# The last weight set in three transfers instead of one, and fifteen small loads behind it on the same queue

## The chip, the cores and the metric

The kernel runs on one core of a Trainium2 chip. A core has a matrix engine (PE), a vector engine (DVE), an activation engine (ACT), a general engine (POOL) and a sync engine (SP). In this kernel SP computes nothing: it is the queue from which nearly all transfers between memory and the core's buffers are issued, one after the other, and sixteen DMA engines carry them out. The metric is the device time of one execution in microseconds (us), lower is better. Before the change it is 218.73 us, the median of two runs (218.32 and 219.14).

## The reference

Two sequences (B = 2) with one token each go through a gated block. The input row is normalised; one branch is attention over a cached window, the other a gated feed-forward part; the output is the input plus the product of the two.

```python
xn = layernorm(x)                                  # x: 2 x 1 x 512
q = (xn @ wq)                                      # 32 heads of 128
k, v = k_cache[:, :, SK-W:, :], v_cache[:, :, SK-W:, :]   # 8 kv heads, window W = 4096
p = softmax(q k^T * 128**-0.5)                     # 4 query heads share a kv head
s = (p v).reshape(2, 1, 4096) @ wo                 # wo: 4096 x 512
z = gelu(xn @ w_in); z1, z2 = halves(z)
g = silu((z1 * (w_sp * layernorm(z2) + b_sp)) @ w_out)
out = x + s * g                                    # 2 x 1 x 512
```

All of it is in 32-bit floats. What has to be read is far larger than what is computed on it: the window of keys and values alone is 64 MB, wq and wo are 8 MB each.

## The kernel before, in words

**Stages.** The feed-forward branch (`win`, `wout`) and the queries (`wqt`) come first. Then eight units follow, one for each kv head; a unit holds 4 MB of keys (`k`) and 4 MB of values (`v`). DVE turns the keys of a unit in four chunks (`turn`), PE multiplies them with the queries (`scores`), and the softmax (`probabilities`) and the product with the values (`values`) follow one or two units later. The outputs of the units are gathered in three sets (`SETS`, line 332): units 0 to 3, units 4 and 5, and units 6 and 7. Each set ends in a small tile `oT` (`spread`), which is the stationary side of the last product, the one with `wo`.

**The last product.** The rows of `wo` are cut like the sets: 4 MB for the first, 2 MB for the second and 2 MB for the third. Lines 479 to 488 load them into two large buffers as *blocks*: a block is one transfer, with its own completion. Before the change the blocks are two of 2 MB for the first set, one of 2 MB for the second, and four of 1 MB, 512 KB, 256 KB and 256 KB for the third. A block of 2 MB gives eight matrix products, one of 256 KB gives one. The first two sets go through `wo_early` (lines 492 to 500), which sums into the four row groups of `part`, 24 products in all (`EARLY = 24`). ACT copies `part` to `parts`, PE folds its groups into `so` with `rowm`, and the blocks of the third set are added to `so` (lines 520 to 527). Then DVE multiplies `so` by the gate and adds the input (`res`, lines 529 and 530), and SP issues the transfer of the result (line 531).

**What sets the order.** `pe`, `dve`, `act` and `sp` are wrapped in `InOrder`: each engine's instructions stay in the order in which the program writes them. For SP that means that a transfer that must wait holds up every transfer written behind it. A transfer on SP waits for three kinds of things. It waits until its buffer may be overwritten: the large buffers are a ring of four, so a load into one waits for the last reader of what was in it, and a load that overwrites what an earlier load wrote waits until that load has landed. It waits for data that it sends out. And it waits for its completion semaphore: the framework has eight for the transfers of SP and ACT and hands them out in turn, so a transfer that takes a semaphore again waits until the transfer eight places earlier has landed. In the built program of before, the last block of `wo` waits for the values of unit 6 to have landed for this reason, and the result's transfer for those of unit 7.

The packets of everything that SP issues go through one queue to the sixteen DMA engines. `x4` (line 108) is the input, loaded early through ACT, and it is the only other small load of a similar kind beside `xs` and the two scalars of `wb1`.

Of the kernel before, what the change touches and what calls it, by code (L numbers as in the profile page):

```python
# [9 lines left out]
F32 = mybir.dt.float32  # L10
# [4 lines left out]
P = 128  # L15
# [27 lines left out]
def kernel(  # L43
# [14 lines left out]
    pe, dve, act, sp = (InOrder(tc, e) for e in (nc.tensor, nc.vector, nc.scalar, nc.sync))  # L58
# [20 lines left out]
    cst = ctx.enter_context(tc.tile_pool(name="cst", bufs=1))  # L79
# [4 lines left out]
    def slot(name, *shape):  # L84
        return ring.tile([P, *shape], F32, tag="slot", name=name)
# [21 lines left out]
    act.dma_start(wb1[:, 1:2], bass.AP(tensor=b_sp.tensor, offset=b_sp.offset, ap=[[1, 1], [1, 1]]))  # L107
    x4 = cst.tile([P, DC], F32, tag="x4", name="x4")
    nc.gpsimd.memset(x4, 0.0)
    by_group = [[DC, G], [D, B], [1, DC]]  # L110
    act.dma_start(x4[0 : P : P // (G * B), :], bass.AP(tensor=x.tensor, offset=x.offset, ap=by_group))

# [330 lines left out]
    def spread_after(p):  # L443
        if p is not None and p.n in ends:
            spread(ends[p.n])
# [33 lines left out]
    blocks = []  # L479
    for first, of in ((0, (0,)), (1, (1, 2))):  # L480
        t = slot(f"wo{first}", 16, D)
        a = 0
        for i in of:
            nj = SETS[i][2]
            for j, n in (((0, 8), (8, 8)), ((0, 8),), ((0, 4), (4, 2), (6, 1), (7, 1)))[i]:
                sp.dma_start(t[:, a : a + n, :], wo_s[i][:, j : j + n, :])
                blocks.append((t[:, a : a + n, :], sets[f"oT{i}"][1], j))
                a += n
    EARLY = 24
    done = 0  # L490

    def wo_early(n):
        nonlocal done
        t, oT, j = blocks[n]
        for a in range(t.shape[1]):
            g = done % G
            pe.matmul(
                part[32 * g : 32 * g + 32, :], oT[:, j + a, :], t[:, a, :], start=(done < G), stop=(done >= EARLY - G)
            )
            done += 1  # L500
# [9 lines left out]
    wo_early(0)  # L510
    gathered(units[-1])
    spread_after(units[-1])
    wo_early(1)
    wo_early(2)
    parts = sb.tile([P, D], F32, tag="o", name="parts", bufs=1)
    act.activation(parts, part, AF.Copy)
    so = bank("so", DC)
    for g in range(G):
        pe.matmul(so[32 * g : 32 * g + 32, :], rowm, parts[:, g * DC : (g + 1) * DC], start=True, stop=False)
    for n in range(3, len(blocks)):  # L520
        t, oT, j = blocks[n]
        for a in range(t.shape[1]):
            for g in range(G):
                pe.matmul(
                    so[32 * g : 32 * g + 32, :], oT[:, j + a, :], t[:, a, g * DC : (g + 1) * DC],
                    start=False, stop=(j + a == oT.shape[1] - 1),
                )
# [32 lines left out]
```

## Time and profile before

| | |
|---|---|
| median of two runs | 218.73 us (218.32 to 219.14) |
| the profiled execution, its own time | 219.13 us |
| its span, first to last instruction | 217.3 us |
| mean granted TensorE clock | 0.772 |
| PE busy | 144.6 us (67%) |
| DVE busy | 104.3 us (48%) |
| ACT busy | 23.9 us (11%) |
| SP's packets, share of 16 DMA engines | 96.3% |
| read from memory | 89.40 MB, 411 GB/s over the span |

The span runs from the first to the last instruction of the core; the time of the execution is 1.8 us more. A row of the timeline gives the start, the busy time, the engine and what is written from what. A row of the chain of work gives the same for the work that ended last, followed back from the end; "DMA" in it is a stretch in which the next instruction waited for a transfer, counted from the transfer's issue. A row of the waits says which engine waited for which result, how long in total, how often, and the longest one. "SPq" is SP's queue of instructions: its busy time on a transfer is the time to issue it, not the transfer itself.

### The profile page before, as it was taken

The page shows a single profiled execution, that of the slowest core. Times are in us where ns is not written, and L with a number is a line of the kernel's source. Part 1 is how long each engine was busy: PE and PEld are TensorE (multiplying, and loading weights), DVE is VectorE, ACT ScalarE, POOL GpSimd, SP SyncE. Part 2 cuts the span into 40 slices and gives each one's busy share as a digit, 9 for nine tenths or more (in the row PEclk, how much of TensorE's full clock was granted, in tenths as well). Part 3 has the DMA queues.
Part 4 walks back from the last instruction along what each step waited for, and adds up shares of the span by engine and source line. Part 5 has one row for each costly group of instructions (what it writes and reads, how often), then busy time and mean ns, then how long its engine had stood idle before and what let it go on. Part 6 is the DMA issues. An engine that isn't in the chain of part 4 may idle for free.

```text
span 217.3 us, 2319 instructions
## 1 busy us (share of the span) xinstructions
PE 144.6 (67%) x970; PEld 55.6 (26%) x970; DVE 104.3 (48%) x162; ACT 23.9 (11%) x60; POOL 3.2 (1%) x16
## 2 busy tenths in 40 slices
PE   0179694826956956974693197459478669979663
PEld 0128521513112212222231122312121122342213
DVE  2511214359459458638709903980684495221101
ACT  5010203100001101011021002102000012021010
POOL 5000000000000000000000000000000000000000
PEclk9998578785597695595599569857855879988969
DMA  7999999999999999999999999999999999999980
GB/s 254 423 434 464 404 464 401 454 410 440 428 434 431 422 440 416 449 410 446 416 452 410 458 407 446 416 440 425 422 442 416 446 416 452 404 413 431 412 323 2
DMA packets 3929, 89.54 MB, mean 412 GB/s; under 512 B 446, under 2 KB 462, under 8 KB 848
## 3 DMA queue, kind: packets, MB, share of 16 engines
q1 hardware_dynamic: 3900, 89.40, 96.3%
q8 instruction: 7, 0.11, 0.2%
q14 instruction: 2, 0.02, 0.0%
q10 hardware_dynamic: 20, 0.01, 0.0%
HBM read 89.40 MB, written 0.00 MB: 411 GB/s over the span
## 4 chain that ended last, share of the span: by engine, by line
DMA 60%; PE 19%; DVE 17%; SPq 1%; issue 1%; ACT 1%; DVEq 0%; ACTq 0%
DMA v<-in_A_v_cache_dram 29%; DMA k<-in_A_k_cache_dram 20%; DVE kt L37 13%; DMA wo<-in_A_wo_dram 11%; PE acc L37 8%; PE s L37 7%; PE part L37 2%; SPq L37 1%; PE so L37 1%; PE pp L37 1%; DVE sm L37 1%; DVE pT L37 1%; DVE qw L37 1%; ACT p L37 0%; DVE mg L37 0%
## 5 line engine op out<-in xcount | busy, mean ns | idle before, releaser
L37 DVE STREAM_TRANSPOSE kt<-k 128x2048 f32<-128x2048 f32 x32 | 72.7, 2293 | 2.4 <-DMA k<-in_A_k_cache_dram 2.4
L37 PE MATMUL acc<-v,pT 128*32 128x512 f32 x256 | 44.9, 857 | 11.1 <-DMA v<-in_A_v_cache_dram 9.8
L37 PE MATMUL s<-kt,qw 128*32 128x512 f32 x256 | 41.0, 683 | 3.7 <-DVE kt L37 3.1
L37 PE MATMUL pp<-p,swap 128*128 128x512 f32 x16 | 12.8, 898 | 21.0 <-ACT p L37 21.0
L37 DVE CUSTOM_DVE_ANT_1 sm<-s,own 128x512 f32<-128x512 f32 x8 | 5.5, 690 | 36.9 <-PE s L37 36.9
L37 PEld LDWEIGHTS acc<-v,pT 128*32 128x32 f32 x256 | 11.5, 159 | 37.4 <-issue 33.4
L37 PEld LDWEIGHTS s<-kt,qw 128*32 128x32 f32 x256 | 9.4, 122 | 32.8 <-issue 21.7
L37 ACT ACTIVATE o<-acc,wd 128x128 f32<-128x128 f32 x30 | 8.7, 368 | 74.0 <-PE acc L37 67.2
L37 PE MATMUL q_ps<-wq,xnT 128*32 128x512 f32 x64 | 10.2, 767 | 5.3 <-DMA wq<-in_A_wq_dram 5.3
L37 ACT ACTIVATE p<-sm,nb 128x512 f32<-128x512 f32 x8 | 5.8, 723 | 68.1 <-DVE nb L37 68.1
L37 PE MATMUL part<-wo,oT 128*32 128x512 f32 x48 | 7.3, 737 | 2.7 <-DMA wo<-in_A_wo_dram 2.7
L37 PEld LDWEIGHTS pp<-p,swap 128*128 128x128 f32 x16 | 3.0, 234 | 21.8 <-ACT p L37 21.8
L37 DVE STREAM_TRANSPOSE pT<-pp 128x512 f32<-128x512 f32 x8 | 5.7, 706 | 6.0 <-PE pp L37 6.0
L37 PE MATMUL z<-win,xnT 128*32 128x448 f32 x32 | 5.2, 820 | 4.6 <-DMA win<-in_B_w_in_dram 4.6
L37 PE MATMUL mo<-mg,same 128*128 128x16 f32 x16 | 3.2, 273 | 7.7 <-DVE mg L37 7.7
L37 DVE TENSOR_REDUCE both<-col 128x32 f32<-128x128 f32 x3 | 0.9, 292 | 13.3 <-PE col L37 13.3
L37 PE MATMUL zT_ps<-rowm,z 128*128 128x2 f32 x28 | 6.6, 370 | 0.0
L37 PEld LDWEIGHTS zT_ps<-rowm,z 128*128 128x128 f32 x28 | 6.5, 325 | 0.0
L37 PEld LDWEIGHTS mo<-l,same 128*128 128x128 f32 x16 | 4.6, 290 | 6.1 <-issue 6.1
L37 DVE TENSOR_TENSOR res<-so,gate 128x128 f32<-128x128 f32 x1 | 0.3, 292 | 10.7 <-PE so L37 10.7
L37 ACT ACT_TABLE_LOAD x4 | 5.1, 1283 | 2.6 <-POOL place L207 2.6
L37 PEld LDWEIGHTS mo<-mg,same 128*128 128x128 f32 x16 | 2.4, 188 | 11.7 <-DVE mg L37 10.9
(105 smaller groups left out, 71.8 us busy)
## 6 DMA issues: line engine op xcount, KB each, us to landing
k<-in_A_k_cache_dram SPq DMA_DIRECT2D x8, 4096.0 KB, 26.6
v<-in_A_v_cache_dram SPq DMA_DIRECT2D x8, 4096.0 KB, 29.9
wq<-in_A_wq_dram SPq DMA_DIRECT2D x2, 4096.0 KB, 24.5
wo<-in_A_wo_dram SPq DMA_DIRECT2D x3, 2048.0 KB, 19.6
win<-in_B_w_in_dram SPq DMA_DIRECT2D x1, 3584.0 KB, 11.4
wout<-in_B_w_out_dram SPq DMA_DIRECT2D x1, 1792.0 KB, 15.2
wo<-in_A_wo_dram SPq DMA_DIRECT2D x1, 1024.0 KB
wo<-in_A_wo_dram SPq DMA_DIRECT2D x1, 512.0 KB
```

The source lines that it names most:

```text
L37: return self.tc.keep_in_program_order(call(*args, **kwargs))
```

## The change

The transfer of the second set of `wo`, one of 2 MB, becomes three of 1 MB, 512 KB and 512 KB. With it the second set is blocks 2 to 4 in place of block 2, and the third set is blocks 5 to 8. The products stay the same in number, shape and order; `wo_early` runs over blocks 1 to 4 and waits for each of them by itself.

Behind the last block of `wo`, SP issues fifteen loads from the input `x` into the first rows of a new tile `marks`: 15 rows of 64 bytes, then 14 rows, and so on down to one. Nothing reads `marks`. All fifteen write from row 0 of the same tile. The result's transfer (line 531 before) comes behind them on SP.

```diff
+    x_in = x
...
-            for j, n in (((0, 8), (8, 8)), ((0, 8),), ((0, 4), (4, 2), (6, 1), (7, 1)))[i]:
+            for j, n in (((0, 8), (8, 8)), ((0, 4), (4, 2), (6, 2)), ((0, 4), (4, 2), (6, 1), (7, 1)))[i]:
                 sp.dma_start(t[:, a : a + n, :], wo_s[i][:, j : j + n, :])
                 blocks.append((t[:, a : a + n, :], sets[f"oT{i}"][1], j))
                 a += n
+    marks = cst.tile([P, 16], F32, tag="marks", name="marks")
+    for n in range(15, 0, -1):
+        sp.dma_start(marks[:n, :], bass.AP(tensor=x_in.tensor, offset=x_in.offset, ap=[[16, n], [1, 16]]))
...
-    wo_early(1)
-    wo_early(2)
+    for n in range(1, 5):
+        wo_early(n)
...
-    for n in range(3, len(blocks)):
+    for n in range(5, len(blocks)):
```

## The prediction

> **What bounds the kernel now.** I read the page first, for the shares; then the end of the chain of work; then SP's own timeline and waits, because everything that the change adds stands on SP.
>
> From the page:
>
> ```profile
> span 217.3 us, 2319 instructions
> ...
> DMA  7999999999999999999999999999999999999980
> ...
> q1 hardware_dynamic: 3900, 89.40, 96.3%
> ...
> HBM read 89.40 MB, written 0.00 MB: 411 GB/s over the span
> ```
>
> The sixteen DMA engines are full in every slice but the first and the last two, and nearly all of it is SP's queue. So the kernel is as long as its transfers, plus what has to happen after the last of them. A change behind the last transfer is paid in full, unless something else is still running then.
>
> What still runs then is shown by the last eleven pieces of the chain that ended last:
>
> ```profile
> 183.28 24.28 DMA wo<-in_A_wo_dram
> 207.55 0.14 issue
> 207.69 3.52 PE part L37 x16
> 211.21 0.02 issue
> 211.23 0.60 ACT parts L37
> 211.84 0.04 issue
> 211.88 2.22 PE so L37 x72
> 214.10 0.02 issue
> 214.12 0.30 DVE res L37
> 214.43 0.02 issue
> 214.45 0.29 DVE res L37
> ```
>
> The second set of `wo`, issued at 183.28, lands at 207.55. PE's eight products with it take until 211.21, the copy and the third set until 214.10, DVE until 214.74. Then the result can go out.
>
> SP's timeline, and SP's waits from 180 us to the end (who waited for whom, in total, times, longest):
>
> ```profile
> 182.36 3.20 SPq L37 DMA_DIRECT2D wo<-in_A_wo_dram  x7
> 214.77 0.69 SPq L37 DMA_DIRECT2D out_dram<-res  x1
> ```
>
> ```profile
> SPq L37 <- DVE res L37: 22.2, 1, 22.2
> ...
> SPq L37 <- DMA v<-in_A_v_cache_dram: 7.0, 1, 7.0
> SPq L555 <- DMA out_dram<-res: 0.7, 1, 0.7
> ```
>
> All seven transfers of `wo` are issued by 185.56 (182.36 + 3.20). Then SP stands 7.0 us, to about 192.5, until the values of unit 7 have landed, and 22.2 us until `res` is there at 214.77. In those 29 us SP has nothing to do, and this is where the fifteen loads go. Whether they fit there is the question of this case.
>
> When `wo` lands, from the group of its transfers, and how the DMA engines end, from a table of short stretches (the last two columns are the engines' share and GB/s):
>
> ```profile
> L37 SPq DMA_DIRECT2D wo<-in_A_wo_dram x7: 336/426/437, 182.4 to 185.1; - x7
> ...
> DMA to landing us min/median/max: 19.6/27.3/27.5
> ```
>
> ```profile
> 207.50:209.00 1.50, 1.31 (x8) 0.45 (x12) 0.00 (x0) 0.00 (x0) 0.00 (x0) 0.50 0.98 400
> 209.00:210.00 1.00, 1.00 (x8) 0.22 (x4) 0.00 (x0) 0.00 (x0) 0.00 (x0) 0.50 1.00 387
> 210.00:211.00 1.00, 1.00 (x8) 0.00 (x0) 0.00 (x0) 0.00 (x0) 0.00 (x0) 0.56 0.63 240
> 211.00:212.00 1.00, 0.29 (x8) 0.12 (x8) 0.00 (x0) 0.60 (x1) 0.00 (x0) 1.00 0.31 115
> 212.00:213.00 1.00, 1.00 (x41) 1.00 (x41) 0.00 (x0) 0.00 (x0) 0.00 (x0) 1.00 0.01 2
> ```
>
> The last block, only 256 KB, is issued at 185.1 and lands 27.5 us later, at 212.6; the engines are empty at 212. A short transfer takes as long as all that was queued in front of it. That is how a first-come queue looks.
>
> **The change part by part.**
>
> *The waits of the added loads.* In the built program each small load waits for its predecessor to have landed, since both write row 0 of `marks`. The first eight also wait for the transfer eight places earlier, whose semaphore they take: the load of 15 rows for the second block of the first set, that of 14 rows for block 2, and so on to that of 8 rows, for block 8, the last of `wo`. The result's transfer waits for `res` alone, but it stands behind all fifteen on SP. What is queued behind the waiting loads is only that transfer; the end of the kernel waits for it, and nobody else does.
>
> *Blocks 6 to 8 of `wo`.* With two more transfers, three blocks now wait for semaphores: block 6 for the values of unit 6, block 7 for those of unit 7 (192.5), block 8 for the first block of the first set. The second 2 MB block lands at about 202.3 (issued at about 182.7, plus the 19.6), the third at 207.55; so 2 MB take some 5 us, and the first lands at about 197.4. Block 8 is issued then, with 15 us of transfers (197.4 to 212.6) still in the queue. The engines stay full, and this costs nothing; the cover would have to shrink by 15 us before it did.
>
> *The second set in three pieces.* Its last piece lands when the whole did, at 207.55, as the bytes in front are the same. But by then PE has done the first six products instead of none: the 1 MB piece lands some 2.5 us earlier, the next some 1.3 us earlier, and PE is idle there. After 207.55 two products of eight are left, 3.52 × 2/8 = 0.9 us. So `part` ends at about 208.6 instead of 211.21 and `parts` at 209.3. From there the third set binds: its last block lands at 212.6, one product is left of it (2.22 us for 36 products of `so`, so four of them 0.25), and PE ends near 213.0 instead of 214.10. Alone this would be worth about 1.1 us. It is worth nothing if SP isn't free at 213.7.
>
> *The fifteen loads.* The first is issued at 202.3 and queues behind `wo`; by the reading above it lands with the end of `wo`, at 212.6. From there, thirteen loads (14 to 2 rows) follow each other, each issued when the one before has landed. The last, one row, is issued and not waited for; then the result goes out. For the step, from the issue of one to the issue of the next, the trace has no row. The nearest are small transfers on an empty queue. From the first microseconds, and from the closing line of the program (its group on SP; count, then min/median/max ns, first and last start):
>
> ```profile
> 0.74 0.55 ACTq L37 DMA_DIRECT2D xs<-in_A_x_dram  x1
> ...
> 1.32 0.24 ACTq L37 DMA_DIRECT2D wb<-in_B_w_sp_dram  x1
> ...
> 2.16 0.68 DVE L37 BATCH_NORM_STATS2 st<-xs 2x6 f32<-2x512 f32 x1
> ```
>
> ```profile
> L555 SPq DRAIN  x3: 7/7/13, 216.6 to 216.9; - x3
> ```
>
> `xs`, two rows read into the core, is issued at 0.74 and its reader starts at 2.16: 1.42 us. The result, eight rows of 512 bytes written to memory, is issued at 214.77, and SP goes on past its landing at 216.6: 1.83 us. In `xs`, 0.55 is the issue; with the shortest issue of a small load, 0.24, it would be 1.42 − 0.55 + 0.24 = 1.11 us. A step is therefore between 1.11 and 1.83 us by the rows, or longer if there is something in a chain of loads that neither row shows. I take 1.65: the kind of transfer is that of `xs`, but the queue is that of the result, where landing takes longer, and an instruction with a wait stands ahead of each load.
>
> The Trainium skill, "DMA: Bandwidth & Descriptors", section "Anatomy of one DMA — SWDGE (gpsimd) path", gives a fixed cost of about 2.0 us for a transfer on another issue path, most of it the confirmation that the last byte has landed. By that price the sum below would end at 243.4. The trace's own two rows are both shorter.
>
> *The sum.* 212.6 (first load landed) + 13 × 1.65 = 21.45, which is 234.05; + 0.45 for the issue of the last load (the transfers of `wo` take 0.43, the row above) is 234.5, where the result is issued. In the trace it is issued at 214.77 and the span ends at 217.3, 2.53 later; so the new span is 237.0, 19.7 more. The profiled execution takes 219.13, 1.83 over its span, which gives **238.9 us**. That execution is at the upper end of the two runs shown, 0.4 above their median; against the median the forecast would be 238.5, and I keep 238.9.
>
> With the two ends of the step: 1.11 gives 212.6 + 14.4 + 0.24 + 2.53 + 1.83 = 231.6; 1.83 gives 212.6 + 23.8 + 0.69 + 2.53 + 1.83 = 241.5. `res` is ready near 213.7 and waits some 20 us for SP, so the gain of the three pieces is not seen.
>
> **The rivals.**
>
> *The small loads pass the bulk.* If the first of them landed soon after its issue at 202.3, the next six would wait for the blocks one by one (their semaphores), and the load of 8 rows for the last block at 212.6. Then seven steps follow (8 to 2 rows) instead of thirteen: 212.6 + 7 × 1.65 + 0.45 + 2.53 + 1.83 = 229.0. For it: fifteen rows of 64 bytes are few packets. Against it: the 256 KB block that landed with all that stood in front of it, 27.5 us after its issue.
>
> *The step is longer than either row.* Rows of 64 bytes, or the waits for two semaphores ahead of a load, might cost what `xs` and the result don't show. At 2.1 us the time is 244.7, at 2.4 us 248.6. For it: `xs` is issued while SP and ACT have just started, and the result is a single transfer, so neither shows a chain. Against it: both are whole transfers from issue to effect.
>
> *Not slower.* The loads are short and might be hidden: SP is free for 29 us and the result isn't ready before 213.7. The point from which this decides is the first load's landing. If it and the others landed at once and cost their issue alone, eight issues of 0.24 would be left after 212.6, the result would go out at 214.5, and the time would be 218.9, no change. With the chain that the program has, 214.77 − 212.6 = 2.2 us would have to hold thirteen steps, 0.17 us each, a tenth of any row. That the three pieces then gain their 1.1 us, to 218.0, also ends here.
>
> **How the numbers follow.** Chain behind `wo` with a step up to 2.0 us: 0.78. The longer step: 0.13. The small loads pass the bulk: 0.06. Not slower: 0.03. The range goes from 233.5 (a step of 1.25 us, nearer the lower bound than I think likely) to 245.0 (a step of 2.1); it takes in most of the first case and about half of the second. A measurement of this kernel tells some 2%, 4.4 us, from no change; all cases but the last are slower by more than that: slower 0.97, same 0.03 with less than 0.01 for faster.
>
> **What the changed profile would show.** Right: SP's timeline has fifteen issues of `marks`, the first near 202.3, the second near 212.6, the rest at equal distances of 1.4 to 1.9 us; SP waits for `marks` some 15 us in total behind `wo`; the DMA line of the page is empty in its last four slices; PE's last product with `wo` ends near 213.0; the chain that ended last runs over `marks`. Wrong in the first rival's way: several issues of `marks` before 212. Wrong in size: equal distances, but of another length. Wrong altogether: the result issued before 216.

## The result and the profile after

The changed kernel takes 234.58 us (median of two runs, 234.44 and 234.73) beside 218.73 us before: 1.071 times as long, with an interval of 1.064 to 1.078. The forecast was 238.9 us, in a range of 233.5 to 245.0. The direction and the mechanism held, and the result lies in the range, near its lower end; the middle was 4.3 us too long.

The page of the changed kernel, the same lines as quoted of before:

```profile
span 232.7 us, 2342 instructions
...
DMA  7999999999999999999999999999999999992000
...
q1 hardware_dynamic: 4428, 89.41, 90.0%
...
HBM read 89.41 MB, written 0.00 MB: 384 GB/s over the span
```

The bytes are the same but for the 8 KB of the loads, and the DMA engines are as full as before for as long as they have work. The span is 15.4 us longer, and the last three slices, 17 us, are empty: the time has been added *behind* the transfers.

SP's own timeline, from the first transfer of `wo` to the end (start, busy time or, where several are merged, the stretch they cover):

```profile
182.27 15.58 SPq L37 DMA_DIRECT2D wo<-in_A_wo_dram  x9
202.42 27.28 SPq L37 DMA_DIRECT2D marks<-in_A_x_dram  x15
229.75 0.67 SPq L37 DMA_DIRECT2D out_dram<-res  x1
```

The result is issued at 229.75 instead of 214.77. Ahead of it stand the fifteen loads, which take SP from 202.42 to 229.70. What SP does in that time is in its waits (whom it waited for, in total, times, longest), shown first. The timeline in short stretches gives single issues; behind the waits stand those of the loads of 15, 14 and 13 rows and of the last two:

```profile
SPq L37 <- DMA marks<-in_A_x_dram: 20.4, 14, 7.7
...
SPq L37 <- DMA wo<-in_A_wo_dram: 11.2, 3, 4.6
SPq L37 <- DMA v<-in_A_v_cache_dram: 7.2, 1, 7.2
```

```profile
202.42 0.41 SPq L37 DMA_DIRECT2D marks<-in_A_x_dram  x1
212.66 0.32 SPq L37 DMA_DIRECT2D marks<-in_A_x_dram  x1
214.00 0.31 SPq L37 DMA_DIRECT2D marks<-in_A_x_dram  x1
...
228.34 0.23 SPq L37 DMA_DIRECT2D marks<-in_A_x_dram  x1
229.48 0.22 SPq L37 DMA_DIRECT2D marks<-in_A_x_dram  x1
```

SP waits for its own small loads fourteen times. The longest wait, 7.7 us, is the second load's for the first, which queues behind `wo`; the second load is issued at 212.66. Then come thirteen steps in 16.82 us (212.66 to 229.48), 1.29 us each, of which 0.22 to 0.32 is the issue and the rest waiting.

The compute, in the meantime, is done early. The last pieces of the chain that ended last:

```profile
212.52 0.47 PE so L37 x8
212.99 0.02 issue
213.02 0.30 DVE res L37
213.32 0.02 issue
213.34 0.29 DVE res L37
```

PE ends at 212.99 instead of 214.10 and `res` is ready at 213.63 instead of 214.74. One thing about this view is to be learned here: it stops at 213.63, 19 us before the end of the span. It follows work and what released it; a queue that only waits for its own transfers behind the last piece of work isn't in it. Who reads this view alone sees a kernel that got 1.1 us faster. The DMA line with its empty last slices and SP's timeline show what happened.

### The profile page after: what moved, and what is told of

Read it like the earlier page. It is cut to its first block, busy times and chain, and to the rows that moved or that the text cites. A ratio compares the mean times of both kernels' runs of the same rounds, so it can differ in the third digit from the quotient of the medians.

```text
span 232.7 us, 2342 instructions
## 1 busy us (share of the span) xinstructions
PE 144.1 (62%) x970; PEld 54.3 (23%) x970; DVE 104.3 (45%) x162; ACT 23.9 (10%) x60; POOL 3.2 (1%) x16
## 4 chain that ended last, share of the span: by engine, by line
DMA 60%; PE 16%; DVE 15%; ACT 1%; issue 1%; DVEq 0%; ACTq 0%
DMA v<-in_A_v_cache_dram 27%; DMA k<-in_A_k_cache_dram 19%; DMA wo<-in_A_wo_dram 13%; DVE kt L37 11%; PE acc L37 8%; PE s L37 6%; PE pp L37 2%; DMA xs<-in_A_x_dram 1%; DVE sm L37 1%; DVE pT L37 1%; ACT p L37 1%; DVE qw L37 1%; DVE mg L37 0%; DVE res L37 0%; PE so L37 0%
## 5 line engine op out<-in xcount | busy, mean ns | idle before, releaser
L37 PE MATMUL acc<-v,pT 128*32 128x512 f32 x256 | 44.0, 842 | 11.1 <-DMA v<-in_A_v_cache_dram 9.9
L37 PE MATMUL pp<-p,swap 128*128 128x512 f32 x16 | 13.4, 931 | 21.0 <-ACT p L37 21.0
L37 PE MATMUL q_ps<-wq,xnT 128*32 128x512 f32 x64 | 10.8, 806 | 6.9 <-DMA wq<-in_A_wq_dram 6.9
L37 PE MATMUL xnT_ps<-ident,xn 2*128 2x2 f32 x4 | 0.6, 253 | 7.3 <-DVE xn L37 7.3
```

The lines of the kernel that those rows point to most:

```text
L37: return self.tc.keep_in_program_order(call(*args, **kwargs))
```

## The experiments

The theory: the loads cost the time because each waits for the one before to land, and the result stands behind them on SP. The rivals: the loads cost by their number or by being there, the pieces of the second set cost something, or only the result's place in the queue matters. Each edit below is against the changed kernel.

**The pieces alone.** The fifteen loads are left out.

```diff
-    marks = cst.tile([P, 16], F32, tag="marks", name="marks")
-    for n in range(15, 0, -1):
-        sp.dma_start(marks[:n, :], bass.AP(tensor=x_in.tensor, offset=x_in.offset, ap=[[16, n], [1, 16]]))
```

> Only the second set in three pieces, without the fifteen loads. Theory (the whole loss is the chain of small loads ahead of the result on SP; the pieces by themselves gain a little): the result goes out at about 213.7 instead of 214.77, so 217.6 to 218.1 us, 0.995 to 0.998 of the kernel before. Rival (the two additional transfers with their semaphore waits cost something themselves): 219.5 us or more.

218.42 us, 0.9986 of the kernel before (0.9956 to 1.0016). The rival is out, since nothing has become slower; but the expected gain isn't there to be measured either, and the time is 0.3 us above what was expected. In its profile (timeline) the pieces do what they should:

```profile
207.59 1.05 PE L37 MATMUL part<-wo,oT 128*32 128x512 f32 x4 [0.21 <-DMA wo<-in_A_wo_dram]
...
212.69 0.43 PE L37 MATMUL so<-wo,oT 128*32 128x128 f32 x8 [0.22 <-DMA wo<-in_A_wo_dram]
...
213.84 0.69 SPq L37 DMA_DIRECT2D out_dram<-res  x1
```

Two products are left of the second set when its last piece lands, PE waits for each block of the third, and the result goes out at 213.84, 0.93 us earlier than in the profiled execution of before. From there the span takes 2.76 us (to 216.6) instead of 2.53. And that execution of before, 219.13 us, was a long one: the median of before in this experiment is 218.66.

**The loads alone.** The second set is one transfer again, with blocks and loops as before.

```diff
-            for j, n in (((0, 8), (8, 8)), ((0, 4), (4, 2), (6, 2)), ((0, 4), (4, 2), (6, 1), (7, 1)))[i]:
+            for j, n in (((0, 8), (8, 8)), ((0, 8),), ((0, 4), (4, 2), (6, 1), (7, 1)))[i]:
...
-    for n in range(1, 5):
+    for n in range(1, 3):
...
-    for n in range(5, len(blocks)):
+    for n in range(3, len(blocks)):
```

> Only the fifteen loads; the second set stays one transfer. Theory: the chain starts at the landing of the last block of wo, which the pieces don't move, so the time is that of the changed kernel within 0.4 us, 234.2 to 235.0; PE's last product is about 1.1 us later than in the changed kernel and nobody notices. Rival (the gain of the pieces comes through beside the chain): 235.5 us or more.

233.91 us, 1.069 of before (1.064 to 1.074): the whole loss without the pieces. It was 0.3 us below what was expected and 0.67 below the changed kernel, which was measured on another occasion; so the two were run once more, on one chip.

> The changed kernel once more, beside the next one on the same chip: 234.2 to 234.8 us.

> The fifteen loads with the second set as one transfer, once more. If the difference of 0.6 us to the changed kernel came from two separate jobs, the two are now within 0.3 us of each other; if the three pieces make the chain later, this one is again 0.5 us or more faster.

234.39 us for the changed kernel (1.0722 of before, 1.0695 to 1.0749) and 234.17 us for the loads alone (1.0718, 1.0685 to 1.0751). The runs of the two overlap, so the 0.67 lay between the two occasions, and with the chain in place the pieces make no difference that can be seen. The first profile of the loads alone has the chain at the same time, although the first load is issued 10 us earlier:

```profile
192.71 36.87 SPq L37 DMA_DIRECT2D marks<-in_A_x_dram  x15
229.62 0.66 SPq L37 DMA_DIRECT2D out_dram<-res  x1
```

```profile
SPq L37 <- DMA marks<-in_A_x_dram: 32.0, 14, 19.5
```

The longest wait has grown from 7.7 to 19.5 us: the first load waits in the queue for the end of `wo`, whenever it is issued.

**A tile for each load.** Nothing is left out; only the common destination goes, and with it the wait for the predecessor.

```diff
-    marks = cst.tile([P, 16], F32, tag="marks", name="marks")
     for n in range(15, 0, -1):
+        marks = cst.tile([P, 16], F32, tag=f"marks{n}", name=f"marks{n}")
         sp.dma_start(marks[:n, :], ...)
```

> The fifteen loads stay where they are on SP, but each writes a tile of its own, so none waits for its predecessor to land; the waits for semaphores eight transfers back stay. Theory (the landings in series are the cost): after the last block of wo lands (212.5) eight issues of 0.25 to 0.28 us are left, the result goes out at about 214.9, 219.5 us. Rival (fifteen more instructions on SP with their semaphores are the cost, whether they wait for each other or not): 230 us or more.

219.91 us, 1.0054 of before (1.0031 to 1.0078). 14.7 of the changed kernel's loss of 15.9 us are gone, with the same fifteen loads of the same size on the same queue. SP's timeline and waits:

```profile
202.50 12.67 SPq L37 DMA_DIRECT2D marks<-in_A_x_dram  x15
215.27 0.67 SPq L37 DMA_DIRECT2D out_dram<-res  x1
```

```profile
SPq L37 <- DMA wo<-in_A_wo_dram: 17.0, 9, 4.6
```

SP no longer waits for `marks`, only for blocks of `wo`, whose semaphores the loads take. The load of 8 rows still waits for the last block, and from there eight issues are left, its own among them; the result goes out 1.4 us later than with the pieces alone. This is the small part of the loss that is SP's own work. It is 0.4 us more than the 219.5 that were expected: from one of these issues to the next it is 0.30 to 0.34 us, not the 0.25 to 0.28 of the issue alone.

**One load instead of fifteen.** Only the one of 15 rows stays.

```diff
-    for n in range(15, 0, -1):
+    for n in (15,):
```

> One small load (15 rows) in place of fifteen, at the same place on SP. Theory (only the landings that follow each other after the end of wo cost): nothing waits for this load before the result is issued, so the time is that of the pieces alone, 218.0 to 218.8 us. Rival (a first small load behind the bulk has a price of its own beside the steps): 219.5 us or more.

218.40 us, 0.9968 of before (0.9932 to 1.0004). A small load behind `wo` costs nothing by itself that can be seen beside the 218.42 of the pieces alone.

```profile
202.61 0.40 SPq L37 DMA_DIRECT2D marks<-in_A_x_dram  x1
213.82 0.66 SPq L37 DMA_DIRECT2D out_dram<-res  x1
```

**Eight loads instead of fifteen.** Those of 15 down to 8 rows stay.

```diff
-    for n in range(15, 0, -1):
+    for n in range(15, 7, -1):
```

> Only the loads of 15 down to 8 rows. Theory (equal steps of 1.29 us per load): seven steps fewer, 7 x 1.28 = 9.0 us, 225.6 us. Rival (a fixed cost of having small loads behind the bulk, with little per load): 230 us or more.

225.75 us (one run; 225.6 was expected). Seven loads fewer are 8.8 us less than the 234.58, 1.26 each: a price per load.

```profile
202.09 18.68 SPq L37 DMA_DIRECT2D marks<-in_A_x_dram  x8
220.83 0.67 SPq L37 DMA_DIRECT2D out_dram<-res  x1
```

**The result from another queue.** The loads stay on SP, the result goes out from ACT.

```diff
-    sp.dma_start(bass.AP(tensor=out.tensor, offset=out.offset, ap=by_group), ...)
+    act.dma_start(bass.AP(tensor=out.tensor, offset=out.offset, ap=by_group), ...)
```

> The result's transfer goes out from ACT instead of from SP, so it stands behind no small load. Theory (the program ends only when SP has come through its chain): the result is issued at 213.7 and lands near 215.7, but the span still ends with SP, about 1 us earlier than in the changed kernel: 233.0 to 234.0 us. Rival (only the result's place in the queue costs): 218 to 220 us.

234.06 us (one run), 0.06 above what was expected. The timeline and SP's waits:

```profile
213.51 0.62 ACTq L37 DMA_DIRECT2D out_dram<-res  x1
213.90 16.16 SPq L37 DMA_DIRECT2D marks<-in_A_x_dram  x13
```

```profile
SPq L559 <- DMA marks<-in_A_x_dram: 0.8, 1, 0.8
```

The result is issued at 213.51, 16 us earlier, and the kernel is hardly faster: its end (line 559) now waits for the last small load. The chain need not stand ahead of anything to cost its length; it is enough that the kernel ends behind it.

**The same chain from an idle engine.** The fifteen loads into one tile are issued from POOL, behind its memsets, at the start of the program.

```diff
+    marks = cst.tile([P, 16], F32, tag="marks", name="marks")
+    for n in range(15, 0, -1):
+        nc.gpsimd.dma_start(marks[:n, :], bass.AP(tensor=x_in.tensor, offset=x_in.offset, ap=[[16, n], [1, 16]]))
     def scores(p, *chunks):
...
-    marks = cst.tile([P, 16], F32, tag="marks", name="marks")
-    for n in range(15, 0, -1):
-        sp.dma_start(marks[:n, :], bass.AP(tensor=x_in.tensor, offset=x_in.offset, ap=[[16, n], [1, 16]]))
```

> The same fifteen loads in the same chain, but issued from POOL, which has nothing else to do after its memsets, so that the result does not stand behind them. Theory: as without the loads, 217.6 to 218.3 us; each step of the chain may be several us, as the loads then share the DMA engines with the bulk, and there are 200 us for them. Rival (small loads disturb the stream of large ones wherever they are issued, or the loads themselves cost the time): 220 us or more.

218.51 us, 0.9981 of before (0.9952 to 1.0009), beside 218.42 without any loads. The upper end of what was expected is passed by 0.2 us, as the pieces alone passed theirs by 0.3; the loads don't show. The group of `marks`:

```profile
L345 POOL DMA_DIRECT2D marks<-in_A_x_dram x15: 518/518/655, 3.7 to 102.3; - x15
...
  DMA marks<-in_A_x_dram: 91.3, 14
...
DMA to landing us min/median/max: 5.5/6.6/7.8
```

The chain is far longer here, from 3.7 to 102.3 us, as each load takes 5.5 to 7.8 us from issue to landing; POOL waits 91.3 us in all. How much of that is sharing the DMA engines with the bulk, and how much the other issuing engine, no run separates. The chain costs nothing, as nobody stands behind it.

**The price of a step, by form.** In place of the fifteen loads, sixteen in one chain: four of one row of 64 bytes, four of two rows of 2 KB (the form of `xs`), four of eight rows of 512 bytes (the form of `x4`, and of the result's transfer), four of sixteen rows of 64 bytes.

```diff
-    marks = cst.tile([P, 16], F32, tag="marks", name="marks")
-    for n in range(15, 0, -1):
-        sp.dma_start(marks[:n, :], bass.AP(tensor=x_in.tensor, offset=x_in.offset, ap=[[16, n], [1, 16]]))
+    marks = cst.tile([P, D], F32, tag="marks", name="marks")
...
+    for dst, ap in rows.values():
+        for _ in range(4):
+            sp.dma_start(dst, bass.AP(tensor=x_in.tensor, offset=x_in.offset, ap=ap))
```

> In place of the fifteen loads, sixteen in one chain: four of one row of 64 bytes, four of two rows of 2 KB (the form of xs), four of eight rows of 512 bytes (the form of x4), four of sixteen rows of 64 bytes. Theory (a step is the issue of the load, which depends on its form, and about 1.02 us from the end of the issue to the next issue): steps of 1.25, 1.57, 1.66 and 1.35 us, 238.4 us in all. Rival (the step is one price of 1.3 us for any small load): equal steps, 15 x 1.3 = 19.5 us and 237.0 us in all.

237.36 us (one run), and neither expectation holds as it stands. The total is near the rival's 237.0, but by luck: shorter and longer steps make up for each other. The issues, from the timeline: the four of one row, and the first two of each other form:

```profile
202.38 0.31 SPq L37 DMA_DIRECT2D marks<-in_A_x_dram  x1
210.72 0.23 SPq L37 DMA_DIRECT2D marks<-in_A_x_dram  x1
211.87 0.22 SPq L37 DMA_DIRECT2D marks<-in_A_x_dram  x1
213.05 0.22 SPq L37 DMA_DIRECT2D marks<-in_A_x_dram  x1
214.19 0.23 SPq L37 DMA_DIRECT2D marks<-in_A_x_dram  x1
215.65 0.23 SPq L37 DMA_DIRECT2D marks<-in_A_x_dram  x1
...
219.78 0.62 SPq L37 DMA_DIRECT2D marks<-in_A_x_dram  x1
221.82 0.56 SPq L37 DMA_DIRECT2D marks<-in_A_x_dram  x1
...
227.59 0.33 SPq L37 DMA_DIRECT2D marks<-in_A_x_dram  x1
229.07 0.32 SPq L37 DMA_DIRECT2D marks<-in_A_x_dram  x1
```

Steps of 1.14 to 1.18 us for one row, 1.34 to 1.46 for two rows of 2 KB, 1.89 to 2.04 for eight rows, 1.38 to 1.48 for sixteen rows of 64 bytes. So the steps aren't equal, and they aren't the issue plus a constant either: from the end of the issue to the next issue it is 0.9 us for one row and 1.4 us for the eight.

## Why the prediction was right, and where it was off

**The bound and the place held.** The DMA engines end at 212, as before, and all the added time lies behind them. Blocks 6 to 8 with their semaphore waits cost nothing, as forecast: SP stands 7.2 us for `v` and then 4.5 us for the first block of `wo` (the rest of the 11.2 us for `wo` is that of the first two loads), and the DMA line stays full until the end of `wo`.

**The chain held.** The first load was expected at 202.3 and issued at 202.42, the second at 212.6 and issued at 212.66. A tile for each load takes most of the loss away, eight loads cost a little less than half of it, the loads alone cost all of it. Of the rivals, that the small loads pass the bulk is out, for a load of fifteen rows, by the 212.66, and by the loads alone, where a first issue 10 us earlier changes nothing. That the loads fit into SP's idle time is out by the result. The longer step is out too, as the step came out shorter than forecast.

**The term that was off is the step.** It was taken as 1.65 us and measured 1.29. The sum with the measured numbers: 212.66 + 16.82 + 0.27 (issue of the last load, to 229.75) + 2.95 (to the end of the span) = 232.7, and 1.74 outside the span gives 234.44. The thirteen steps make 4.6 us of the difference to the forecast, the last issue 0.2, and the closing part takes 0.4 back: its 2.53 came from one execution, the shortest; in the other profiles in which the result leaves from SP it is 2.7 to 3.3. The two bounds of the step, 1.11 and 1.83, held it; the choice between them was too high. The experiment on forms shows why: I raised the 1.42 of `xs` because of the result's 1.83, as a matter of SP's queue. On SP itself, though, two rows like those of `xs` have steps of 1.34 to 1.46, and eight rows like those of the result, loaded instead of stored, have 1.89 to 2.04: the form makes the difference. That two rows take just what `xs` took is in part luck, since of the 1.42 of `xs` 0.55 was the issue on ACT, and the issue on SP is 0.23. The added loads are nearer to the two rows. The issue, put at 0.45, is 0.22 to 0.32.

The fixed cost of about 2.0 us of the Trainium skill ("DMA: Bandwidth & Descriptors", "Anatomy of one DMA — SWDGE (gpsimd) path") would have given 243.4 us. As a price of one step on SP the traces don't bear it out for these loads: a step is 1.14 to 1.48 us for all forms but the eight rows, and only for those, at 1.89 to 2.04, is it near. The Trainium skill states it for the other issue path, so this doesn't contradict it, and beside the bulk that path took 5.5 to 7.8 us here. What the prediction quotes from the Trainium skill, that most of this price is the confirmation, the traces don't show for loads on SP either: from the end of a load's last packet to the next issue it is 0.27 to 0.40 us in the experiment on forms.

**The pieces held in the trace and not in the time.** `part` was to end at 208.6, and its last product in the changed kernel ends at 208.54:

```profile
207.49 1.05 PE L37 MATMUL part<-wo,oT 128*32 128x512 f32 x4 [0.22 <-DMA wo<-in_A_wo_dram]
```

PE ends at 212.99, forecast 213.0. But "alone worth about 1.1 us" was read from one execution of before. The eight products that the pieces spread out took 3.52 us there, at a granted clock of 0.50; with one transfer for the set, in the profile of the loads alone, the chain has

```profile
207.51 2.94 PE part L37 x16
...
211.13 2.48 PE so L37 x72
```

and PE's end is 213.61 instead of 214.10. The short stretches of the same profile show the difference in the clock (the third column from the right), which at first is still 0.77:

```profile
207.50:209.00 1.50, 1.49 (x12) 0.60 (x16) 0.00 (x0) 0.00 (x0) 0.00 (x0) 0.77 0.99 397
209.00:210.00 1.00, 1.00 (x8) 0.00 (x0) 0.00 (x0) 0.00 (x0) 0.00 (x0) 0.50 0.92 355
```

In the second profile of the loads alone the eight products took 2.44 us, at a clock of 0.90 until 209, and PE ended at 213.48. So with one transfer PE's end varied by 0.6 us from execution to execution, as the clock was higher ahead of it or behind: the eight products took 3.52, 2.94 and 2.44 us, the later ones 2.22, 2.48 and 2.98. The pieces alone have PE's end at 213.16, 0.3 to 0.9 us earlier. The end from the result's issue on was 0.2 us longer there. The measured gain, 0.24 us by the medians, fits what is left, and is also within what no change would give. In the changed kernel the clock is 1.00 from 207.5 to 213; whether the pieces bring that about is not shown.

**Of the signs named,** the fifteen issues and the idle end of the DMA line came (three empty slices and one at 2, not four empty ones). The distances were 1.14 to 1.39 us and not 1.4 to 1.9, and SP's waits behind `wo` were 12.7 us (20.4 − 7.7) and not 15. That the chain that ended last would run over `marks` was wrong: the view ends with the last piece of compute.

## What to carry to other kernels

In this program a transfer that overwrites what an earlier transfer wrote waits for its landing, and a row of such transfers is a chain whose price is the number of steps times the time of one. Here that time went by the form more than by the bytes: 4 KB in two rows took 1.34 to 1.46 us, 4 KB in eight rows 1.89 to 2.04. Where it stands decides the rest: behind the last bulk transfer it is paid in full, even if the result leaves by another queue, while from an idle engine beside the bulk a chain of 100 us was free. To price a step, take the row of a transfer of the same form before one of the same queue.

## What the runs showed of the hardware that was not expected

A one-row load came through the end of the bulk earlier than one of fifteen rows. In the experiment on forms the second load is issued at 210.72, 1.9 us before the last block's product starts in the same profile's chain:

```profile
197.47 15.08 DMA wo<-in_A_wo_dram
212.55 0.04 issue
212.59 0.47 PE so L37 x8
```

In the changed kernel the first load, of 15 rows, let the second go only at 212.66. The Trainium skill ("DMA: Bandwidth & Descriptors", "Why a DMA increments its semaphore by 16 and not by 1") says that a transfer from SP runs on the largest number of engines, sixteen at most, that divides the slowest dimension above size one of both its sides, and that each engine which it uses adds its own count to the completion semaphore. For fifteen rows that is fifteen engines. The packet records of the traces agree. A load of fourteen rows leaves 28 packets, one of sixteen rows 32: for each row one of 64 bytes and one of 4. One of eight rows, whose slowest dimension is four, leaves eight of 512 bytes and four of 4. One of a single row leaves one of 64 bytes and one of 4, which fits one engine.

The same records show when the rows came through. In the experiment on forms the 64 bytes of the first load move at 210.06, while packets of `wo` go on until 212.05. In the changed kernel the fifteen rows of the first load move one after the other from 209.92 to 212.05, and the load has landed only with the last of them. So the engines don't end together (a share of 0.63 and then 0.31 in the last two microseconds of transfers, in the table of the prediction), and a load of one row waits for one of them only. The records don't name the engine of a packet, so which one was early is not seen.

Where the time of a step goes can be read there too, behind the end of `wo`. From the start of the issue to the first packet it is 0.83 to 0.93 us for three of the forms and 1.30 to 1.40 us for the eight rows; the packets take 0.31 us at most; from the end of the last packet to the next issue it is 0.27 to 0.40 us in all four forms. What makes the eight rows dearer lies ahead of their first packet, in the issue and behind it, and not in the landing.

The issue of a small load on SP grows with its rows, from 0.22 us for one row to 0.32 for fourteen, and the form matters more: 0.52 to 0.62 us for eight rows spread over the partitions.
